# One kernel, several edits: w_in loaded and cast without a change of partitions, batch 1's queries in two loads, and a new order of small matmuls around chunk 0

## The chip, the cores and the metric

The kernel runs on one core of a Trainium2 chip. The metric is device time in microseconds (us). A core has five engines that run side by side, each through its own list of instructions in order: TensorE (PE in the profile; PEld is its weight load), VectorE (DVE), ScalarE (ACT), GpSimd (POOL) and SyncE (SP, which here only issues DMAs). An instruction waits on semaphores for what it needs, and everything behind it on its engine waits with it.

## What is computed

Two layers in a row, from inputs in float32. The first is a linear attention with cosine weights, for 8 batches, 8 heads, 576 positions and 64 features:

```python
r = np.maximum(x, 0.0); phi = np.concatenate([r * c, r * s], axis=-1)   # c, s: cos and sin of the position
q_p, k_p = phi(q), phi(k)
kv  = np.einsum('bhsf,bhsd->bhfd', k_p, v);  z = np.sum(k_p, axis=2)
num = np.einsum('bhsf,bhfd->bhsd', q_p, kv)
den = np.einsum('bhsf,bhf->bhs', q_p, z)[..., None] + 1e-06
attn = num / den
```

The second takes the 4608 tokens of 512 features that come out (heads side by side) through two matrices with a gate between them:

```python
h = x @ w_in                                   # 4608x512 by 512x2048
g = h * (1.0 / (1.0 + np.exp(-beta * h)))
out = g @ w_out                                # 2048x512
```

## The kernel before

**Attention.** A batch's q, k and v are each loaded as 128 partitions x 4 x 9 x 64 (`load_raw`, line 76). A partition holds nine neighbouring positions n of one head; the 128 partitions are 64 groups of positions for each of two heads (g), and the four blocks j are the other factor of the heads. Pairs of blocks make up a half jp of the heads. DVE or ACT takes the relu of q (`q_relu`) and k (`k_relu`) into bfloat16 and multiplies v by cosine and sine into `vb` (`v_scale`). The queries are turned, features to partitions, by PE transposes (`q_turn_pe`, batches 0 and 1) or by a DMA transpose on SP (`q_turn_dma`). Of the turned queries there are two sets: `qts`, a copy, and `qs`, the copy times the tangent of the position (`tan_mul`, with the table `tanr`), so that cosine and sine parts share one relu. PE then forms kv with 72 small matmuls of 64x64 tiles (`kv_mm`, L276), copied by `kv_take`, and the numerators and denominators with eight small matmuls for each n and jp (`num_mm`, L297). `x_rden` and `x_mul` divide (DVE, or ACT in `x_mul_act`), and the quotients are turned into `xt` by PE (`x_turn_pe`, L356) or DMA (`x_turn_dma`).

**The two matrices.** The tokens are cut into nine chunks of 512; a chunk is 8 blocks of 64 tokens, block 9b + n being position group n of batch b. So chunk 0 needs n = 0 to 7 of batch 0, chunk 1 needs n = 8 of batch 0 and n = 0 to 6 of batch 1. For each chunk PE makes 16 groups of 128 features (`h_mm`, L386, four matmuls of 512 columns that run over mi, the quarters of the 512 inputs: mi 0 and 1 come from half jp 0 of the heads, mi 2 and 3 from jp 1), ACT applies Silu out of PSUM (`h_act`, L394), and the second matrix follows: chunk 0 by 64 wide matmuls (`o_mm`, L544), chunk 1 by a seven-product scheme with half as wide matmuls (`o_fast`, L563), chunks 2 to 8 by orders that a planner has written (`ORDERS`), which the change leaves as they are. The scheme of seven products needs sums of weights T (`w_sums`) and of activations S1 to S4 (`g_sum`, L406) from DVE.

**Weights.** w_in comes in four stages of 512 columns, each 128 partitions x 4 x 512 float32 in one of four staging buffers; the partition of a row of w_in there is not the one that `xt` needs, since a 128-row block holds two g. `cast_win` (line 105) therefore casts to bfloat16 in pieces of 64 partitions, from partitions g*64 to partitions jj*64, on DVE, GpSimd or ACT. w_out follows in four stages through the same buffers (`load_w`), cast and scaled by 1/beta in 16 blocks (`cast_out`).

**The order.** All of it is written by hand, and each engine takes its instructions as the program issues them. DMAs of inputs are all issued on SP in one queue: q, v, k of batch 0 in halves, w_in stages 0 to 3, w_out 0 and 1, then batch 1's v, k, q, then w_out 2 and 3. Lines 685 to 754 are the attention for the first eight position groups of batch 0, with matmuls on zeros (`warm_pe`, `warm_long`) that keep PE occupied while data arrive. A loop over 32 slots follows (line 854): slots 0 to 15 are chunk 0's h groups, 16 to 23 the first half of the second matrix (eight of the 16 blocks, four at a time for each of four token rows), 24 to 31 the other half, one block at a time for all four. The dictionary `early` (line 807) hangs other work behind a slot: behind slot 4 the matmuls for n = 8 of batch 0 and `rest()`, which issues the casts and loads above; behind 22 batch 1's kv; behind 23 (`second`) the PE transposes of batch 1's queries; behind 25 and 26 the numerators for n = 0 to 6, one half of the heads each (a "seven": 56 small matmuls); behind 28 and 29 their turns. The loop of chunk 1 (line 882) has, behind slot 0, the numerators for n = 7 and 8 of batch 1, the relus and DMA turn of batch 2's queries, and the cosine half of its v; behind slot 4 its k, behind 6 the sums T, behind 10 its kv. Then come batch 3's query relus on ACT and their DMA turn (lines 899 to 901), and then `o_fast` (911), whose first step for each pair of rows is a product "1" and a copy by ACT, "c1" (L602), out of the bank in which product "6" goes on.

```python
    for slot in range(16):
        h_group(1, slot)
        if slot == 0:
            num_rest()
            att_q(2)
            v_half(2, 0)
...
    q_relu(3, 0, "act")
    q_relu(3, 1, "act")
    q_turn_dma(3)
...
    x, y = o_fast(1, 0, (2, 5, 4)), o_fast(1, 1, (3, 7, 6))
    ops(x, "1 c1")
```

Of the kernel before, what the change touches and what calls it, by code (L numbers as in the profile page):

```python
# [10 lines left out]
FP32 = mybir.dt.float32  # L11
# [5 lines left out]
P = 128  # L17
NQ = 9
# [4 lines left out]
def kernel(  # L23
# [52 lines left out]
    def load_raw(b, name, j0=0, j1=4):  # L76
        js = slice(j0, j1)
        src = {"q": q, "k": k, "v": v}[name][b]
        nc.sync.dma_start(  # L79
            out=raw_tile(b, name)[:, js].rearrange("q j n d -> q j (n d)"),  # L80
            in_=src.rearrange("(j g) (p n) d -> (g p) j (n d)", g=2, n=NQ)[:, js, :])
# [9 lines left out]
    w_in_v = moe_w_in.rearrange("(j p) f -> p j f", p=P)  # L91
# [3 lines left out]
    def load_w(kind, i, step=4):  # L95
# [3 lines left out]
        for a in range(0, 4, step):  # L99
            if kind == "out":  # L100
                nc.sync.dma_start(out=st[:, a : a + step], in_=w_out_v[:, 4 * i + a : 4 * i + a + step, :])
                continue
            nc.sync.dma_start(out=st[:, a : a + step], in_=w_in_v[:, a : a + step, i * 512 : (i + 1) * 512])

    def cast_win(i, gj, eng="dve", f0=0, f1=512, jps=slice(0, 2)):

        g, jj = gj
        o = win[i].rearrange("q (jp g) f -> q jp g f", g=2)[jj * HP : (jj + 1) * HP, jps, g, f0:f1]
        a = stages["in", i].rearrange("q (jp jj) f -> q jp jj f", jj=2)[g * HP : (g + 1) * HP, jps, jj, f0:f1]
# [16 lines left out]
    GJ = [(0, 0), (0, 1), (1, 0), (1, 1)]  # L126

    load_raw(0, "q", 0, 2)
    load_raw(0, "q", 2, 4)
    beta16 = const.tile([JT, P], FP32, name="beta16")  # L130
    nc.scalar.dma_start(out=beta16, in_=moe_beta.rearrange("(j p) -> j p", p=P))
# [63 lines left out]
    def q_relu(b, jp, eng="dve", n0=0, n1=NQ):  # L195
        return relu(qb[:, jp, n0:n1].rearrange("q n (j d) -> q j n d", j=2),
                    raw_tile(b, "q")[:, 2 * jp : 2 * jp + 2, n0:n1], eng)

    def k_relu(b, j0=0, j1=4, eng="dve", n0=0, n1=NQ):
        relu(rk.rearrange("q n j d -> q j n d")[:, j0:j1, n0:n1], raw_tile(b, "k")[:, j0:j1, n0:n1], eng)  # L200

    def v_scale(b, cs, jp=None, n0=0, n1=NQ, eng="dve"):
        t = (cos9, sin9)[cs]
        rv = raw_tile(b, "v")
        js = slice(0, 4) if jp is None else slice(2 * jp, 2 * jp + 2)
# [21 lines left out]
    def q_turn_pe(b, jp, bank, hold=False):  # L227

        parts = ((0, 0, 5), (1, 5, NQ))
# [40 lines left out]
    def kv_mm(b, jp, bank, jjs=(0, 1)):  # L270
        t = kv_out(jp, bank)
        for n in range(NQ):
            for jj in jjs:
                for g in range(2):
                    hs = slice(g * HP, (g + 1) * HP)
                    nc.tensor.matmul(  # L276
                        t[jj * HP : (jj + 1) * HP, g], lhsT=rk[hs, n, 2 * jp + jj, :],
                        rhs=vb[hs, n, 2 * jp + jj].rearrange("q s e -> q (s e)"),
# [10 lines left out]

    def num_mm(b, n, jp, bank, slot):  # L290

        for cs in range(2):
            for jj in range(2):
                rows = slice(jj * HP, (jj + 1) * HP)
                for g in range(2):
# [3 lines left out]
                        lhsT=(qts[b % 2], qs_of(b))[cs][rows, jp, n, cols],  # L299
# [385 lines left out]
    warm_pe(58, 48)  # L685
# [7 lines left out]
    for bank, n0, n1 in ((6, 0, 5), (7, 5, NQ)):  # L693
        nc.vector.tensor_copy(tanr[:, n0:n1, :].rearrange("q n p -> q (n p)"), ps[:, bank, 0 : (n1 - n0) * HP])
# [47 lines left out]
    for gj, eng in zip(GJ, ("pool", "dve", "pool", "dve")):  # L742
        cast_win(0, gj, eng, jps=slice(0, 1))
    for gj, eng in zip(GJ, ("act", "pool", "pool", "pool")):
        cast_win(0, gj, eng, jps=slice(1, 2))
# [10 lines left out]
    def cast_halves(i, fs=(0, 256)):  # L756
        for f in fs:
            for gj in GJ:
                cast_win(i, gj, "pool" if i > 1 and gj == GJ[3] else "dve", f, f + 256)

    cast_halves(1)

    def rest():

        cast_halves(2)
        cast_halves(3)
        x_mul(x_rden(2, 0, 8, NQ, (0, 1)), 8, NQ)
# [4 lines left out]
        load_raw(1, "q")  # L772
        load_w("out", 2, 2)
        load_w("out", 3, 2)
        x_turn_dma(0, 8, 9)
# [5 lines left out]
        q_relu(1, 0)  # L781
        q_relu(1, 1, n1=5)
# [6 lines left out]
    takes = []  # L789

    def second():

        takes.append(q_turn_pe(1, 0, 4, hold=True))
        takes.append(q_turn_pe(1, 1, 6, hold=True))
        cast_out(8)
        takes[0]("act", 0)
        takes[0]("dve", 1)
        cast_out(9, "a")
        takes[0]("dve", 0)
        takes[0]("act", 1)  # L800
        cast_out(10)
# [290 lines left out]
```

## Time and profile before

| | |
|---|---|
| median of 3 runs | 274.07 us (273.53 to 274.22) |
| the profiled execution | 274.44 us, of which the span is 272.7 us |
| PE busy | 265.3 us, 97% of the span |
| DVE, ACT, POOL busy | 224.0, 188.4, 68.3 us |
| DMA | 54.00 MB, mean 198 GB/s; 388 GB/s from 18.7 to 37.9 us |
| granted TensorE clock, mean | 0.998 |

The profile is one execution recorded by the hardware. Its timeline lists instructions with start, length, engine, line, shape and, in brackets, the idle time of the engine before them and what ended it; the chain of waits follows the work that ended last back from the end; the windows give each engine's busy time in a stretch. A PE row's length runs to the modelled end of its last matmul, so distances between starts say more about PE than lengths do. "L386" is line 386 of the kernel before.

### The profile page before, as it was taken

The page shows a single profiled execution, that of the slowest core. Times are in us where ns is not written, and L with a number is a line of the kernel's source. Part 1 is how long each engine was busy: PE and PEld are TensorE (multiplying, and loading weights), DVE is VectorE, ACT ScalarE, POOL GpSimd, SP SyncE. Part 2 cuts the span into 40 slices and gives each one's busy share as a digit, 9 for nine tenths or more (in the row PEclk, how much of TensorE's full clock was granted, in tenths as well). Part 3 has the DMA queues.
Part 4 walks back from the last instruction along what each step waited for, and adds up shares of the span by engine and source line. Part 5 has one row for each costly group of instructions (what it writes and reads, how often), then busy time and mean ns, then how long its engine had stood idle before and what let it go on. Part 6 is the DMA issues. An engine that isn't in the chain of part 4 may idle for free.

```text
span 272.7 us, 8970 instructions
## 1 busy us (share of the span) xinstructions
PE 265.3 (97%) x3712; PEld 206.8 (76%) x3712; DVE 224.0 (82%) x596; ACT 188.4 (69%) x384; POOL 68.3 (25%) x89
## 2 busy tenths in 40 slices
PE   8899999999899999999999999999999999999994
PEld 8554455455784588888888888888888888888883
DVE  5989969499989889789989997899589768757852
ACT  4778777796419656899489966996696179428920
POOL 1444000510078000660085009300840060000001
PEclk9999999999999999999999999999999999999999
DMA  6999999999969999994589439943600570015005
GB/s 237 374 395 383 392 390 319 379 201 336 284 130 311 240 348 226 240 313 103 147 216 370 92 58 223 332 71 62 181 2 2 61 185 1 2 27 130 0 2 155
DMA packets 50681, 54.00 MB, mean 198 GB/s; under 512 B 31232, under 2 KB 31760, under 8 KB 50640
## 3 DMA queue, kind: packets, MB, share of 16 engines
q1 hardware_dynamic: 47504, 45.55, 59.1%
q0 software_dynamic: 2784, 7.61, 9.6%
q8 instruction: 29, 0.48, 0.7%
q10 hardware_dynamic: 352, 0.27, 0.4%
q14 instruction: 12, 0.10, 0.1%
HBM read 36.71 MB, written 9.44 MB: 169 GB/s over the span
## 4 chain that ended last, share of the span: by engine, by line
PE 85%; DVE 9%; DMA 3%; SPq 1%; issue 1%; ACT 1%; DVEq 0%
PE ps L621 32%; PE ps L511 27%; PE ps L386 10%; PE ps L544 5%; PE ps L563 4%; PE ps L297 3%; DMA raw_v<-in_v_dram 3%; PE ps L276 3%; DVE vb L219 1%; DVE xs L319 1%; DVE qs L223 1%; SPq L79 1%; DVE S L406 1%; DVE rk L193 1%; DVE qb L193 0%
## 5 line engine op out<-in xcount | busy, mean ns | idle before, releaser
L537 POOL DMA_DIRECT2D out_dram<-o_sb x58 | 33.9, 591 | 147.3 <-ACT o_sb L658 86.3
L420 ACT ACTIVATE g_t<-ps,beta 128x512 bf16<-128x512 f32 x96 | 60.3, 702 | 1.4 <-PE ps L511 1.3
L621 PEld LDWEIGHTS <-S 128*128 128x128 bf16 x448 | 43.4, 98 | 5.2
L511 PE MATMUL ps<-w_stage 128*128 128x256 bf16 x288 | 46.6, 272 | 0.1
L386 PE MATMUL ps<-xt,win 128*128 128x512 bf16 (+1 forms) x196 | 42.8, 375 | 0.1
L511 PEld LDWEIGHTS <-w_stage 128*128 128x128 bf16 x384 | 37.3, 98 | 5.1 <-issue 0.2
L487 DVE TENSOR_TENSOR ps<-ps,p 128x256 f32<-128x256 f32 x74 | 30.5, 428 | 8.6 <-PE ps L511 3.0
L394 ACT ACTIVATE g_t<-ps,beta 128x512 bf16<-128x512 f32 x48 | 32.3, 688 | 7.2 <-PE ps L386 7.1
L621 PEld LDWEIGHTS <-g_t 128*128 128x128 bf16 x336 | 32.3, 98 | 4.5 <-ACT g_t L420 0.4
L386 PEld LDWEIGHTS <-win 128*128 128x128 bf16 x196 | 18.7, 98 | 21.1 <-issue 0.5
L511 PE MATMUL ps<-xt,win 128*128 128x256 bf16 x192 | 32.9, 273 | 0.0
L511 PEld LDWEIGHTS <-win 128*128 128x128 bf16 x288 | 28.0, 98 | 3.4
L621 PE MATMUL ps<-wout,g_t 128*128 128x256 bf16 x224 | 28.9, 273 | 0.0
L406 DVE TENSOR_TENSOR S<-g_t 128x512 bf16<-128x512 bf16 (+1 forms) x66 | 25.7, 418 | 3.3 <-ACT g_t L420 1.7
L480 ACT COPY ps<-ps 128x256 f32<-128x256 f32 x62 | 22.6, 383 | 7.5 <-PE ps L621 4.0
L217 ACT ACTIVATE vb<-raw_v,sin 128x256 bf16<-128x256 f32 (+1 forms) x58 | 26.0, 503 | 1.5 <-DMA raw_v<-in_v_dram 1.5
L621 PE MATMUL ps<-T,S 128*128 128x256 bf16 x224 | 26.6, 273 | 0.0
L621 PE MATMUL ps<-wout,S 128*128 128x256 bf16 x224 | 26.4, 273 | 0.0
L319 DVE TENSOR_TENSOR xs<-ps,rden 128x768 bf16<-128x768 f32 (+4 forms) x26 | 22.8, 884 | 0.9 <-DVE rden L312 0.2
L223 POOL TENSOR_TENSOR qs<-qt,tanr 128x1152 bf16<-128x1152 bf16 x6 | 14.3, 2387 | 27.4 <-PE ps L563 21.0
L658 ACT COPY o_sb<-ps 128x512 f32<-128x512 f32 x11 | 6.3, 587 | 20.1 <-PE ps L621 20.1
L487 DVE TENSOR_TENSOR ps<-ps,u 128x256 f32<-128x256 f32 x36 | 15.3, 427 | 5.3 <-PE ps L511 3.3
(112 smaller groups left out, 414.7 us busy)
## 6 DMA issues: line engine op xcount, KB each, us to landing
raw_v<-in_v_dram SPq DMA_DIRECT2D x7, 1152.0 KB, 9.7
raw_k<-in_k_dram SPq DMA_DIRECT2D x7, 1152.0 KB, 9.5
raw_q<-in_q_dram SPq DMA_DIRECT2D x7, 1152.0 KB, 7.4
out_dram<-o_sb POOLq DMA_DIRECT2D x58, 128.0 KB, 4.5
w_stage<-in_moe_w_in_dram SPq DMA_DIRECT2D x3, 1024.0 KB, 12.8
w_stage<-in_moe_w_out_dram SPq DMA_DIRECT2D x2, 1024.0 KB, 7.9
w_stage<-in_moe_w_out_dram SPq DMA_DIRECT2D x4, 512.0 KB, 11.9
out_dram<-o_sb SPq DMA_DIRECT2D x10, 128.0 KB, 2.4
```

The costliest lines, as they stand in the source:

```text
L217: got = nc.scalar.activation(o, a, AF.Copy, scale=t[:, n : n + 1])
L223: return eng.tensor_tensor(dst.rearrange("q n (g p) -> q n g p", g=2), src.rearrange("q n (g p) -> q n g p", g=2), tanr[:, n0:n1].unsqueez ...
L319: nc.vector.tensor_tensor(o.rearrange("q j n s d -> q j (n s) d"), nv[:, :, a:z, :, 0:D].rearrange("q j n s d -> q j (n s) d"), rden[:, :, ...
L386: nc.tensor.matmul(ps[:, h_bank(c, jt), i * 64 : (i + w) * 64], lhsT=win[jt // 4][:, mi, (jt % 4) * P : (jt % 4 + 1) * P], rhs=xt[:, i : i ...
L394: return nc.scalar.activation(gs[c, jt // 4][:, jt % 4], ps[:, h_bank(c, jt)], AF.Silu, scale=beta[:, jt : jt + 1])
L406: return nc.vector.tensor_tensor(o, l, r, op=op)
L420: return nc.scalar.activation(gs[c, jt // 4][:, jt % 4], bank, AF.Silu, scale=beta[:, jt : jt + 1])
L480: return nc.scalar.copy(at("a", 0), at("b", 0))
L487: nc.vector.tensor_tensor(dst, at("b", 0), st["p5"], op=ALU.add)
L511: nc.tensor.matmul(dst, lhsT=l[:, g], rhs=r[:, :, g * HP : (g + 1) * HP], start=start and g == 0, stop=g == 1, skip_group_check=True)
L537: (eng or own).dma_start(out=out_v[bb, n][:, m0:m1], in_=o_sb[hf * HP : (hf + 1) * HP, m0:m1])
L621: nc.tensor.matmul(dst, lhsT=l(i), rhs=r[:, i], start=start and i == 0, stop=i == order[-1], skip_group_check=True)
```

## The change

- **w_in.** A half jp now holds heads blocks j = jp and jp + 2, no longer 2jp and 2jp + 1 (`heads`, and the slices in `q_relu`, `k_relu`, `v_scale`, `kv_mm`). With that, a partition of a staged w_in row is the one that `xt` needs, if rows are taken as (jj, mi, d): each load becomes two, for 64 partitions each, and a cast runs over all 128 partitions. Stage 0 is cast by mi (GpSimd, DVE, ACT, GpSimd), stages 1 to 3 in four pieces of 128 columns each, all on DVE.
- **Batch 1's queries** come in two loads (n below 7, then 7 and 8), between halves of w_out stages 2 and 3. Only n = 0 to 6 are turned by PE, 7 and 8 by two DMA transposes and two GpSimd products behind slot 31.
- **Bursts and turns of chunk 0.** The matmuls for n = 8 of batch 0 move from slot 4 to slot 22, directly before batch 1's kv; batch 1's query turn moves from 23 to 25, both sevens to 27, their turns to 30 and 31. The loads of batch 2 and the last w_out casts move with them.
- **Chunk 1.** The first halves of groups 0 to 3 are issued ahead of the loop. The numerators n = 7 and 8 of batch 1 move from slot 0 to slot 10, directly before batch 2's kv, and their division behind it; batch 2's query relus move from slot 0 to slot 4.
- **Batch 3's query relus** and turn move behind the two "1 c1" of `o_fast`.
- **The start.** A DMA on ACT's queue reads 8 numbers of each of 16 rows spread over v of batch 0 ("early rows of v"), ahead of beta's. 74 matmuls on zeros stand first, not 58. The table `tanr` is copied by ACT, not DVE.

The core of the diff:

```diff
+    def heads(j0, j1):
+        if j1 - j0 == 4:
+            return slice(0, 4)
+        at = 2 * (j0 % 2) + j0 // 2
+        return slice(at, at + 1) if j1 - j0 == 1 else slice(at, 4, 2)
...
-            nc.sync.dma_start(out=st[:, a : a + step], in_=w_in_v[:, a : a + step, i * 512 : (i + 1) * 512])
+            for jj in range(2):
+                nc.sync.dma_start(out=st[jj * HP : (jj + 1) * HP, a : a + step],
+                                  in_=w_in_v[jj, :, a : a + step, i * 512 : (i + 1) * 512])
...
-        o = win[i].rearrange("q (jp g) f -> q jp g f", g=2)[jj * HP : (jj + 1) * HP, jps, g, f0:f1]
-        a = stages["in", i].rearrange("q (jp jj) f -> q jp jj f", jj=2)[g * HP : (g + 1) * HP, jps, jj, f0:f1]
+        o, a = win[i][:, mi0:mi1, f0:f1], stages["in", i][:, mi0:mi1, f0:f1]
...
+    touch = const.tile([2 * H, 8], FP32, name="touch")
+    nc.scalar.dma_start(out=touch, in_=v[0].rearrange("h (s r) d -> (h s) r d", s=2)[:, 0, 0:8])
     nc.scalar.dma_start(out=beta16, in_=moe_beta.rearrange("(j p) -> j p", p=P))
...
-        parts = ((0, 0, 5), (1, 5, NQ))
+        parts = ((0, 0, 5), (1, 5, NQ)) if b == 0 else ((0, 0, 4), (1, 4, 7))
...
-    warm_pe(58, 48)
+    warm_pe(74, 48)
...
-        nc.vector.tensor_copy(tanr[:, n0:n1, :].rearrange("q n p -> q (n p)"), ps[:, bank, 0 : (n1 - n0) * HP])
+        nc.scalar.copy(tanr[:, n0:n1, :].rearrange("q n p -> q (n p)"), ps[:, bank, 0 : (n1 - n0) * HP])
...
-    for gj, eng in zip(GJ, ("pool", "dve", "pool", "dve")):
-        cast_win(0, gj, eng, jps=slice(0, 1))
-    for gj, eng in zip(GJ, ("act", "pool", "pool", "pool")):
-        cast_win(0, gj, eng, jps=slice(1, 2))
+    for mi, eng in enumerate(("pool", "dve", "act", "pool")):
+        cast_win(0, mi, mi + 1, eng)
...
-        load_raw(1, "q")
-        load_w("out", 2, 2)
-        load_w("out", 3, 2)
-        x_turn_dma(0, 8, 9)
+        load_w("out", 2, 2, 0, 2)
+        load_raw(1, "q", n1=7)
+        load_w("out", 2, 2, 2, 4)
+        load_w("out", 3, 2, 0, 2)
+        load_raw(1, "q", n0=7)
+        load_w("out", 3, 2, 2, 4)
...
+    def eighth():
+        for jp in range(2):
+            num_mm(0, 8, jp, 4, jp)
+        kv_mm(1, 0, 6)
+        kv_mm(1, 1, 6)
+        kv_take((0, 1), 6, "act")
+        x_mul(x_rden(4, 0, 8, NQ, (0, 1)), 8, NQ)
...
     early = {
-        4: lambda: (num_mm(0, 8, 0, 2, 0), num_mm(0, 8, 1, 2, 1), rest()),
+        4: rest,
         15: lambda: (v_scale(1, 1, n1=8, eng="act"), k_relu(1, 2, 4, "act")),
-        22: lambda: (kv_mm(1, 0, 6), kv_mm(1, 1, 6), kv_take((0, 1), 6, "act"), q_relu(1, 1, "act", 5)),
-        23: second,
-        25: lambda: (num_seven(0, 4), x_mul(x_rden(4, 0, 0, 7, (0,)), 0, 7), cast_out(13)),
-        26: lambda: (num_seven(1, 6), x_mul(x_rden(6, 0, 0, 7, (1,)), 0, 7)),
-        28: lambda: x_turn_pe(1, 0, 7, 4, ("act",), (0,)),
-        29: lambda: x_turn_pe(1, 0, 7, 5, ("dve",), (1,)),
+        22: eighth,
+        25: turn,
+        27: sevens,
+        30: lambda: x_turn_pe(1, 0, 7, 4, ("act",), (0,)),
+        31: lambda: (x_turn_pe(1, 0, 7, 5, ("dve",), (1,)), q_rest()),
     }
...
+    for jt in range(4):
+        h_mm(1, jt, (0, 1))
     for slot in range(16):
-        h_group(1, slot)
+        if slot < 4:
+            h_mm(1, slot, (2, 3))
+            h_act(1, slot)
+        else:
+            h_group(1, slot)
         if slot == 0:
-            num_rest()
-            att_q(2)
             v_half(2, 0)
...
         if slot == 4:
+            att_q(2)
             k_all(2)
...
         elif slot == 10:
+            num_rest()
             kv_all(2, eng="act")
+            x_rest()
...
-    q_relu(3, 0, "act")
-    q_relu(3, 1, "act")
-    q_turn_dma(3)
...
     ops(x, "1 c1")
     one_sums(1)
     ops(y, "1 c1")
+    q_relu(3, 0, "act")
+    q_relu(3, 1, "act")
+    q_turn_dma(3)
```

`turn` holds the turn of batch 1's queries, their takes, the remaining relus and the loads of batch 2's v, q and k; `sevens` both sevens and their divisions; `q_rest` the two DMA transposes and two GpSimd products for n = 7 and 8; `rest` as before, without what has moved. The small matmuls for n = 8 of batch 0 read a copy of their tangent queries that GpSimd makes (`qs_last`), as batch 1's turn writes the tile that holds them.

## The prediction

> **What bounds the kernel now.** I read the busy time by windows first, then TensorE's (PE's) timeline, then the chain of waits. The windows divide the span where PE's behaviour changes; their columns are stretch, length, busy time (and instructions) of PE, PEld, DVE, ACT, POOL, then the granted clock, DMA share and GB/s.
>
> ```profile
> 18.70:37.90 19.20, 19.20 (x110) 8.96 (x110) 17.10 (x42) 15.90 (x27) 2.91 (x4) 1.00 1.05 388
> 37.90:52.00 14.10, 14.09 (x291) 8.15 (x291) 8.62 (x17) 9.53 (x17) 1.19 (x2) 1.00 1.06 356
> 52.00:69.10 17.10, 17.10 (x292) 9.45 (x290) 16.96 (x34) 13.97 (x23) 3.54 (x7) 1.00 1.06 290
> 69.10:70.20 1.10, 0.14 (x12) 0.15 (x2) 1.03 (x4) 1.10 (x3) 0.00 (x0) 1.00 1.05 396
> 70.20:269.00 198.80, 198.72 (x2696) 168.59 (x2695) 164.99 (x462) 135.84 (x291) 52.94 (x60) 1.00 0.59 148
> ```
>
> From 18.7 us on PE never rests, but for one hole at 69.1. So only three things can pay: an earlier 18.7, that hole, and PE work or slow changes inside "busy" time. An engine made faster elsewhere pays nothing. DMA is full (1.05 to 1.06) until 70, so data come at a fixed pace and PE, if it gets ahead, can run into them.
>
> The hole, in PE's and ACT's timelines (start, length, what, idle before and what ended it):
>
> ```profile
> 65.91 1.91 PE L563 MATMUL ps<-wout,g_t 128*128 128x256 bf16 x16
> 70.15 1.91 PE L563 MATMUL ps<-T,S 128*128 128x256 bf16 x16 [0.96 <-ACT p L602]
> ...
> 67.62 2.22 ACT L192 ACTIVATE qb<-raw_q 128x1152 bf16<-128x1152 f32 x2 [0.82 <-DMA raw_q<-in_q_dram]
> 69.74 0.63 ACT L602 COPY p<-ps 128x256 f32<-128x256 f32 x2
> ```
>
> ACT waits for batch 3's queries, takes 2.22 for their relus, and only then does the two copies for which PE stands.
>
> Inside busy time the slow changes show in the starts. PE, chunk 1's first group and the rest:
>
> ```profile
> 50.36 1.03 PE L386 MATMUL ps<-xt,win 128*128 128x512 bf16 x4
> 51.70 8.81 PE L386 MATMUL ps<-xt,win 128*128 128x512 bf16 x40
> ```
>
> The first-to-first distance is 1.34; four 512-wide matmuls at 0.216 are 0.86, so the burst of 32 small matmuls (64x64 tiles, num_mm) between them cost 0.48. The chain of waits prices them:
>
> ```profile
> 22.07 0.25 PE ps L297 x16
> ...
> 42.98 0.58 PE ps L297 x56
> 43.56 0.97 PE ps L544 x4
> 44.53 0.18 PE ps L297 x5
> 44.70 0.01 issue
> 44.71 0.61 PE ps L297 x40
> ```
>
> 56 cost 0.58 there and 16 cost 0.25: 0.0083 each. So 32 are worth 0.27, and **0.21 of the 0.48 is going into 64x64 tiles and back**. The first 56 confirm it: 41.09 to 43.49 less eight wide ones (1.73) leaves 0.67 = 0.46 + 0.21. The second 56, 43.49 to 45.25 less four wide ones, leaves 0.90: **0.22 more, a stall**, in which the rows at 44.53 and 44.71 are split; its qs pieces come from DVE at 44.0.
>
> **The change, part by part.**
>
> *Merged bursts.* Before there are six small bursts from 22 to 62: n=8 of batch 0 (slot 4), kv of batch 1, two sevens, n=7,8 of batch 1, kv of batch 2. After, n=8 stands directly before kv, the two sevens together, n=7,8 directly before the second kv: three bursts. Gain 3 x 0.21 = **0.63**. A change between two kinds of small matmul is not shown alone; bounds 0 and 0.21 each, I take 0, as they share the tile size.
>
> *The second sevens' stall* (**0.22**) goes: they now run after slot 27, two slots (1.73) behind the transposes instead of two split ones, and the takes are 384 and 512 wide, not 640 and 512. By ACT's and DVE's rows (0.5 to 0.6 each) the last take ends near 44.6, PE comes near 44.7. What is late next is ACT's cast of row block 15, near 47.2; PE wants it near 48.3.
>
> *Four transposes fewer* in batch 1's turn (14, not 18): 18 start 0.0565 apart, so **0.23**. They become two DMA transposes on SP and two GpSimd products (2.39 for 1152 columns, so some 0.5 for 256), issued behind loads of batch 2, needed only after slot 10 of chunk 1 near 59. Batch 2's k, ahead of them, lands near 54. On SP they delay batch 2's turn, whose relus end near 54 anyway.
>
> *The hole* (**1.00**: 2.39 from the first of 144 small matmuls to 70.15, less 1.24 for them and 0.15 to leave). The relus of batch 3 stand behind both copies now. Next in line is S2 (L406). DVE's run of 14.7 us before S1, from 51.92 to 66.66, began behind n=7,8; now it can begin near 50.1, when the last xt copy is done, so S2 ends near 67.7 and PE comes near 68.1. Batch 3's DMA turn is issued near 69.3 against 69.86, so the DMAs behind it on SP are no later.
>
> *Four half-groups of chunk 1 first*: same matmuls. ACT gets its Silus 0.43 apart but takes 0.69, and falls 1 to 2 us behind; four banks cover that.
>
> *Casts.* DVE's 22 of 0.50 between 10 and 35 become 13, with as many columns each. DVE had 1 to 2 us in hand for each w_in stage, so this is worth 0, except one: two casts end at 16.83, behind num_mm, and one will not; at most 0.1.
>
> *The start.* Rows of DVE's timeline:
>
> ```profile
> 7.12 1.42 DVE L223 TENSOR_TENSOR qs<-ps,tanr 128x512 bf16<-128x512 bf16 x2
> 9.16 1.34 DVE L209 TENSOR_TENSOR vb<-raw_v,ps 128x1152 bf16<-128x1152 f32 x1
> 12.25 1.35 DVE L209 TENSOR_TENSOR vb<-raw_v,ps 128x1152 bf16<-128x1152 f32 x1 [0.19 <-DMA raw_v<-in_v_dram]
> ```
>
> DVE is busy from 7.12 to 15.6 but for 0.19, so earlier rows of v can pay 0.19 at most, though v's first half lands 2.70 behind q's (4.84, 6.30, 9.00, 10.44 for q, q, v, k). The touch costs: a second issue on ACT (0.45) shifts the table load, sine and tangent, so the tangent transposes start near 4.0, not 3.56. The 16 more dummies, 0.040 apart, end at 3.95 and are hidden by this; the second ones behind it end 0.45 later, the first turn at 7.54, not 7.08, and DVE's product starts at 7.58. That is 0.46 on DVE's run; its 0.19 of idle time takes a part. Moving tanr to ACT (idle 2.10 there) frees DVE earlier, where it only waits. Less the cast's 0.1, PE's dense work begins **0.17 later** (0.46 - 0.19 - 0.10). Bounds: 0.5 later (the full delay), 0.3 earlier (no delay, idle and cast both gone).
>
> *Queries in two loads, casts of w_out reordered*: q's 7 rows land near 39.8 behind k (36.1) and half a w_out stage; turned near 41.8. Hidden by 1 us.
>
> *w_in by two loads of 64 partitions.* No load of before has 64 partitions, only stores. In the packet records, a 2,048-byte packet of a w_in load takes 0.085 at the median, one of SP's 64-partition stores 0.151; GpSimd's 64-partition stores take 0.159 for 4,096 bytes, the full pace. So between 0 and 0.066 for each of the 128 packets that an engine has of w_in: **0 to 8.4 us** late for all that lands behind. I take 0, by the many GpSimd stores and because a load, unlike the stores after 240, has the next load queued behind it, so engines may be in different halves; both ends stay in the range.
>
> **Sum.** -0.63 - 0.22 - 0.23 - 1.00 + 0.17 = -1.91. The profiled execution took 274.44 (span 272.7 and 1.74 around it): 272.53. It lies 0.37 above the median of the runs, 274.07; on that, **272.2 us** (272.16).
>
> **Rivals.**
>
> *A, slower: half pace on w_in.* At 0.151 k of batch 1 lands 8.4 late, at 44.5; its relu and the burst, at 37.90 against a landing of 36.13, follow at 46.2, 8.3 late; the gains behind it (1.0, 0.23, 0.22, 0.42) stay: 274.07 + 8.3 - 1.9 = 280.5. It decides from 0.3 (PE's slack at this burst) plus 2 us, so from packets of 0.103 on the average. For it: SP's store rows; against: GpSimd's. [...] Mixed halves give 274 to 277.
>
> *B, gains lost in waits.* PE comes earlier to data of unchanged pace: k's relu ends at 37.56, PE wants it near 37.8. If it lands 0.5 later, or the start's 0.5 is paid whole, or small kinds do cost their change, 0.6 to 1.2 is lost: 272.9 to 273.5.
>
> *C, the start is bound by landings after all*: v's excess of 1.26 over its neighbours' 1.44 then comes off, 270.9 to 271.6. DVE's rows speak against it.
>
> **Chances.** Forecast (271.6 to 272.9) 0.52, A 0.22, B 0.20, C 0.06. A measurement of this kernel can tell some 0.3%, 0.8 us. Faster by more: the forecast, C and half of B, 0.68; within: the other half, 0.10; slower: A, 0.22. The range of 8 in 10 leaves out C's end and most of A: 271.3 to 275.5.
>
> **What will show it.** Right: no hole of PE near 68, w_in packets of 0.085, stage 3 landed by 25, PE busy from 18.8 on, three small bursts. Wrong: the last w_in landing past 27, a wait of PE for rk or win casts, the dense stretch beginning past 19.2.

## The result and the profile after

| | before | after |
|---|---|---|
| median | 273.77 us (6 runs, 273.28 to 274.22) | 288.64 us (6 runs, 287.16 to 290.33) |
| after / before | | 1.0544 (95%: 1.0504 to 1.0584) |
| the profiled execution | 274.44 us, span 272.7 | 289.28 us, span 287.5 |
| PE busy | 265.3 us, 97% | 267.7 us, 93% |
| idle time of PE, up to the end of its last matmul | 3.7 us | 15.7 us |

Ratios compare fast runs, those within 1.5% of the fastest of the same kernel, while medians hold all runs (`e6_buffer` has one run outside, `e15_half` two).

The change makes the kernel 14.9 us slower. PE has hardly more to do; it waits. The windows of the kernel after (stretch, length, busy time of PE, PEld, DVE, ACT, POOL, granted clock, DMA share, GB/s); the second, third and last line begin at the same places of its work as the first, second and last that the prediction shows of before:

```profile
9.00:18.70 9.70, 6.55 (x213) 3.90 (x213) 7.00 (x17) 5.97 (x15) 3.10 (x3) 0.82 1.04 269
18.70:46.30 27.60, 21.32 (x120) 9.48 (x118) 12.03 (x34) 16.43 (x30) 0.96 (x2) 1.00 1.06 294
46.30:58.40 12.10, 12.06 (x248) 7.16 (x249) 7.91 (x18) 8.34 (x16) 0.00 (x0) 1.00 1.07 342
58.40:78.16 19.76, 16.89 (x173) 8.08 (x170) 13.80 (x26) 13.70 (x25) 6.67 (x10) 1.00 1.02 258
78.16:82.37 4.21, 3.45 (x160) 2.86 (x160) 4.21 (x8) 2.88 (x5) 0.00 (x0) 1.00 1.05 400
82.37:284.00 201.63, 199.55 (x2696) 168.42 (x2696) 168.27 (x468) 135.91 (x291) 52.98 (x60) 1.00 0.60 146
```

The second line, up to batch 1's kv, is 27.6 long where before had 19.2, with 6.3 idle. Its DMA share is as full as before's (1.06 and 1.05), but the DMAs move 294 GB/s, not 388: each is busy all the time and brings less. The fourth line, chunk 1, has 2.9 more of idle time. The last line is 2.8 longer than before's: 1.4 is one wait (at 120.85, for DVE), 0.6 lies behind PE's last matmul.

What PE waits for stands in DVE's timeline: the casts of w_in for stages 1, 2 and 3, then batch 1's k, each begin when a landing allows it (the brackets: idle time before, and what ended it):

```profile
24.79 1.43 DVE L121 CAST win<-w_stage 128x512 bf16<-128x512 f32 x4 [5.23 <-DMA w_stage<-in_moe_w_in_dram]
29.52 1.43 DVE L121 CAST win<-w_stage 128x512 bf16<-128x512 f32 x4 [3.29 <-DMA w_stage<-in_moe_w_in_dram]
34.35 1.43 DVE L121 CAST win<-w_stage 128x512 bf16<-128x512 f32 x4 [3.40 <-DMA w_stage<-in_moe_w_in_dram]
...
45.49 0.76 DVE L199 TENSOR_SCALAR rk<-raw_k 128x1152 bf16<-128x1152 f32 x1 [0.29 <-DMA raw_k<-in_k_dram]
...
67.24 1.91 DVE L199 TENSOR_SCALAR qb<-raw_q 128x1152 bf16<-128x1152 f32 x2 [5.50 <-DMA qt<-qb]
```

The last piece of w_in lands at 34.26 (24.51 before), batch 1's k at 45.47 (36.13). The last line is a second cause, which the prediction did not see: batch 2's query relus write `qb`, and batch 1's positions 7 and 8 lie in that buffer until two DMA transposes have read them. DVE stands still for 5.50 us.

The hole that the change was to close is closed; ACT's timeline has both copies ahead of the relus:

```profile
79.23 0.38 ACT L612 COPY p<-ps 128x256 f32<-128x256 f32 x1 [0.83 <-PE ps L573]
80.10 0.37 ACT L612 COPY p<-ps 128x256 f32<-128x256 f32 x1 [0.50 <-PE ps L573]
80.37 2.22 ACT L198 ACTIVATE qb<-raw_q 128x1152 bf16<-128x1152 f32 x2
```

### The profile page after: what moved, and what is told of

Same layout as the page of the kernel before. It is cut to its first block, busy times and chain, and to the rows that moved or that the text cites. A ratio compares the mean times of both kernels' runs of the same rounds, so it can differ in the third digit from the quotient of the medians.

```text
span 287.5 us, 9001 instructions
## 1 busy us (share of the span) xinstructions
PE 267.7 (93%) x3724; PEld 206.3 (72%) x3724; DVE 218.5 (76%) x585; ACT 189.0 (66%) x388; POOL 65.9 (23%) x85
## 4 chain that ended last, share of the span: by engine, by line
PE 65%; DMA 24%; DVE 7%; issue 1%; SPq 1%; ACT 1%; DVEq 0%
PE ps L631 27%; PE ps L521 26%; DMA w_stage<-in_moe_w_in_dram 10%; PE ps L396 6%; DMA w_stage<-in_moe_w_out_dram 5%; DMA qt<-qb 4%; DMA raw_v<-in_v_dram 3%; PE ps L573 3%; PE ps L306 2%; PE ps L283 2%; DVE qs L230 1%; DMA raw_q<-in_q_dram 1%; DVE vb L226 1%; DVE S L416 1%; SPq L86 1%
## 5 line engine op out<-in xcount | busy, mean ns | idle before, releaser
L230 POOL TENSOR_TENSOR qs<-qt,tanr 128x1152 bf16<-128x1152 bf16 (+1 forms) x8 | 16.7, 2090 | 31.2 <-DVE den L318 20.8
L226 DVE TENSOR_SCALAR vb<-raw_v,cos 128x256 bf16<-128x256 f32 x63 | 20.7, 378 | 2.8 <-DMA raw_v<-in_v_dram 2.8
```

What stands on the lines that cost most here:

```text
L226: got = nc.vector.tensor_scalar(o, a, scalar1=t[:, n : n + 1], scalar2=None, op0=ALU.mult)
```

## The experiments

All times are medians, each against the kernel before on the same chip (273.35 to 273.66).

### Is it the 64 partitions, or the number of loads?

`e1_halves` is before with its w_in loads cut in two by partitions; `e2_columns` has as many loads, all over 128 partitions.

```diff
e1  -  nc.sync.dma_start(out=st[:, a : a + step], in_=w_in_v[:, a : a + step, ...])
    +  for hf in range(2):
    +      ph = slice(hf * HP, (hf + 1) * HP)
    +      nc.sync.dma_start(out=st[ph, a : a + step], in_=w_in_v[ph, a : a + step, ...])
e2  -  load_w("in", 0, 2)  ...  load_w("in", i)
    +  load_w("in", 0, 1)  ...  load_w("in", i, 2)
```

> The kernel before with one edit: every load of w_in is split into two, one for partitions 0 to 63 and one for 64 to 127; casts, order and the rest are untouched. Theory 1 (loads of 64 neighbouring partitions run at half pace, and that is the first loss): the 2,048-byte packets of w_in take 0.15 to 0.16 us instead of 0.085, the last piece of w_in lands near 33 to 34 instead of 24.5 and batch 1's k near 44 to 45.5 instead of 36.1, kv of batch 1 starts 7 to 9 later, and the time is 280 to 283. Theory 2 (the number of loads costs, not their partitions): slower too, but the packets keep 0.085 and gaps between loads appear. Theory 3 (the new order of small matmuls and loads is what costs): packets near 0.085 to 0.10 and a time within 1 us of before, 274 to 275.

> The kernel before with twice as many loads of w_in, as many as in the changed kernel, each over all 128 partitions and half of the row blocks. Theory 1 (64 partitions): nothing changes, packets 0.085, last piece of w_in near 24.5, time 274.0 +- 0.5. Theory 2 (number and size of the loads): as slow as the kernel with loads by 64 partitions, 280 to 283. Theory 3 (the new order): 274.0 +- 0.5, as theory 1.

Measured: `e1_halves` 283.71, 1.0372 (1.0349 to 1.0394), 10.4 slower; `e2_columns` 273.50, 1.0001 (0.9991 to 1.0010). One line of windows from each, for 18 to 24 us; first e1, then e2:

```profile
18.00:24.00 6.00, 5.62 (x50) 2.78 (x41) 2.48 (x8) 3.81 (x8) 1.83 (x3) 0.83 1.05 216
```

```profile
18.00:24.00 6.00, 5.99 (x52) 3.11 (x50) 5.03 (x12) 5.01 (x9) 1.41 (x3) 1.00 1.05 387
```

The DMA share is the same, the rate is 216 against 387. The 2,048 packets of w_in (2,048 bytes each) take 0.153 at the median in e1, 0.084 in e2, 0.085 in before, 0.160 in the kernel after. The last piece of w_in lands at 33.93 in e1, k at 45.14. So the partitions alone cost 10.4, a little over the upper end of theory 1, and the number of loads nothing.

`e5_ports` asks which 64 partitions.

```diff
+    load(t1, 0, P, 0, 2); load(t1, 0, P, 2, 4)          # 128 partitions
+    load(t2, 0, HP); load(t3, 0, HP); load(t2, HP, P); load(t3, HP, P)
+    load(t4, 32, 96); load(t5, 32, 96)
+    for t in (t6, t7): load(t, 0, HP); load(t, HP, P, eng=nc.scalar)
```

> The kernel before, and behind its end seven extra loads' worth of w_in into free buffers, so its time has no meaning and only the packets and landings of the extra loads are read; all are 0.5 MB per load. In order on SP: two loads over 128 partitions, two over partitions 0 to 63, two over 64 to 127, two over 32 to 95, then two pairs of 0 to 63 on SP and 64 to 127 on ACT's queue. Theory 1a (half pace, because 64 neighbouring partitions as such share something with the next load of the same half): packets 0.085 for 128 partitions and 0.15 for all three kinds of halves; 0.085 to 0.10 for the pairs on two queues if both halves then run side by side, 0.15 if they do not. [...] Theory 2 (number or size of loads): all eight kinds alike.

Its windows while the extra loads run; in order 128 partitions, 0 to 63, 64 to 127 (SP's and ACT's queue both had that half at work), 32 to 95:

```profile
273.00:274.00 1.00, 0.00 (x0) 0.00 (x0) 0.00 (x0) 0.00 (x0) 0.00 (x0) 0.50 1.05 408
275.00:279.00 4.00, 0.00 (x0) 0.00 (x0) 0.00 (x0) 0.00 (x0) 0.00 (x0) 0.50 1.05 203
283.00:287.00 4.00, 0.00 (x0) 0.00 (x0) 0.00 (x0) 0.00 (x0) 0.00 (x0) 0.50 1.06 203
292.00:293.00 1.00, 0.00 (x0) 0.00 (x0) 0.00 (x0) 0.00 (x0) 0.00 (x0) 0.50 1.03 381
```

The packets take 0.084, 0.169, 0.171 and 0.085. It isn't the number 64: the middle 64 partitions run at nearly the pace of 128 (381 GB/s against 408), either half runs at half (203). What makes the halves differ from the middle is not shown. So theory 1a, 0.15 for all three kinds, fails by the 0.085 of the middle, and theory 2 by the 0.169 and 0.171 of the halves; the "64 neighbouring partitions" of the expectations, and the 64 of the prediction, hold for the two halves, not for any 64. (The pairs on two queues did not meet: ACT's halves were through when SP's began.)

`e12_twoq` (the changed kernel, batch 1's queries as before, upper halves of w_in on ACT's queue) lets the halves run together. As built, it puts the upper halves of all four stages there; its expectation names stages 0 and 1 only.

```diff
-            for jj in range(2):
-                nc.sync.dma_start(...)
+            for jj in jjs:
+                (nc.sync, nc.scalar)[jj].dma_start(...)
...
     k_relu(0, 0, 2, "act", 0, 5)
+    load_w("in", 1, jjs=(1,))
```

> The changed kernel with batch 1's queries as before, and with the upper halves (partitions 64 to 127) of w_in's stages 0 and 1 loaded on ACT's queue beside the lower halves on SP's; stages 2 and 3 keep both halves on SP. Theory 1 (two halves at a time use the DMAs whole, one at a time only half): packets near 0.085 to 0.10 while both queues run, stage 1 complete near 19 to 21 where the changed kernel has 24.7, then half pace again for stages 2 and 3, 5 us late instead of 9.8; 280 to 283. Rival (a load of 64 partitions is slow whatever runs beside it): packets 0.15 throughout, stage 1 complete near 24, 285 to 287.

Measured: 283.32, 1.0345 (1.0313 to 1.0377). Two of its windows:

```profile
18.00:20.00 2.00, 0.03 (x4) 0.06 (x1) 0.43 (x1) 0.13 (x1) 0.86 (x1) 0.88 1.10 221
...
24.00:26.00 2.00, 2.00 (x15) 1.44 (x14) 1.25 (x4) 1.07 (x2) 0.00 (x0) 0.67 1.06 350
```

From 18 to 20 nearly all packets are of ACT's queue, the upper half (202 against 6), and take 0.162; from 24 to 26 both halves are at work (144 and 198), at 0.096. So halves help each other when both are moving, but the two queues drift apart, and in the first of these windows one half moves almost alone. Stage 1 is complete at 24.66, not by 21: the time is 0.3 over theory 1's range, and its landings are late. Of the 5.2 that this kernel gains on the kernel after, some 2.9 are batch 1's queries (below), so the second queue saves about 2 of w_in's 10.

`e7_one` and `e8_onebuf` were to load the changed kernel's rows over 128 partitions at once (`e8_onebuf` with the repair of `e6_buffer`, below).

```diff
-            for jj in range(2):
-                nc.sync.dma_start(out=st[jj * HP : (jj + 1) * HP, a : a + step], in_=w_in_v[jj, :, a : a + step, ...])
+            for mi in range(a, a + step):
+                nc.sync.dma_start(out=st[:, mi], in_=w_in_v[:, :, mi, ...])      # (jj d) against jj, d
```

> The changed kernel with one edit: each quarter mi of a w_in stage is loaded by one load over all 128 partitions (16 loads of 256 KB), no longer by two loads of 64 partitions for several quarters; the same numbers land in the same places, and all else stands. Theory 1 (loads of 64 neighbouring partitions run at half pace): packets 0.085, the last piece of w_in lands near 25 instead of 34.3, and the time is that of the kernel without the w_in edits, 277.5 to 279, 10 less than the changed kernel. Rival (the rows of w_in in the order jj, mi, d are slow to read, however many partitions a load has): packets 0.15, 287 to 289.

> The changed kernel with both repairs: one load of 128 partitions for each quarter of a w_in stage, and batch 1's last query relus in a place of their own. If the two losses are apart from each other, 275.0 to 276.5, some 12 to 13 below the changed kernel and still 2 above before; what then stays is the start, the wait of PE with no releaser near 20, and order. If chunk 1's loss was only a result of late data, the second repair brings nothing on top of the first, 277.5 to 279.

Measured: 349.02 and 347.29, 1.2764 and 1.2698: a miss by 70 us, and no test of theory 1. The window of e7:

```profile
20.00:60.00 40.00, 13.28 (x43) 5.22 (x43) 3.41 (x11) 7.34 (x13) 0.96 (x2) 0.57 0.13 51
```

The packets take 0.084 again, but the DMA share is 0.13, as two busy engines of 16 would give, and the rate 51 GB/s. The source's first dimension is jj there, with two steps. That this dimension leaves two engines is the author's reading; no run changes it alone.

### Chunk 1: the two DMA transposes

`e3_rest` has every edit but those of w_in.

> The changed kernel with w_in loaded and cast as before (128-partition loads, the old pairing of head blocks, casts of 64 partitions); all other edits stand. Theory 1, with the wait found in the changed kernel's trace (batch 2's query relus stand on DVE behind the two DMA transposes that read the same buffer, and those behind loads of batch 2 on SP): packets 0.085, w_in landed near 24.5, PE dense from about 18.8, and DVE idle before batch 2's first query relu for 1 to 4 us; 272.2 if PE does not notice that, 273.5 to 275.5 if it does. Theory 3 (the order, whatever the loads): 283 to 287, with the wait as long as in the changed kernel, 5.5.

Measured: 278.26, 1.0198 (1.0166 to 1.0230). That is between the ranges of the two theories. So w_in is 10 of the 14.9, and the other edits cost 4.9 where the prediction gave them a gain of 1.9. `e6_buffer` gives batch 1's positions 7 and 8 a place of their own; `e9_queries` undoes the whole part.

```diff
e6  -  q_relu(1, jp, "act", 7)
    +  relu(q_last[:, jp]..., raw_tile(1, "q")[..., 7:], "act")          # q_last lies in S3
    -  ... in_=qb[:, jp, 7:]..., transpose=True
    +  ... in_=q_last[:, jp]..., transpose=True
e9  -  load_raw(1, "q", n1=7)  ...  load_raw(1, "q", n0=7)
    +  load_raw(1, "q")                    # behind k; q_turn_pe turns all nine positions
    -  31: lambda: (x_turn_pe(...), q_rest()),
    +  31: lambda: x_turn_pe(...),
```

> The kernel that has all edits but those of w_in (278.3), with the relus of positions n = 7 and 8 of batch 1's queries put into a place of their own, in a buffer of sums that is not yet in use, so that batch 2's query relus need not wait until the two DMA transposes have read them. If that wait is what the order costs in chunk 1: DVE starts batch 2's queries when they land, near 53.1, not at 56.9, the four holes of PE at 60.4, 67.4, 70.0 and 71.7 (1.7 us together) go or nearly go, and so do slower steps between them; 275.6 to 276.8. If DVE is late for another reason (GpSimd's two products beside it, batch 2's k landing at 56.5), the holes stay and the time stays within 0.6 of 278.3.

> The kernel with all edits but those of w_in (278.3), with batch 1's queries also as before: one load behind k, all nine positions turned by PE (18 transposes), no DMA transposes and GpSimd products for n = 7 and 8. Theory 1 now: the two extra DMA transposes are what chunk 1 pays for, first by the buffer they read, then (with a buffer of their own, 277.7) because batch 2's k lands at 57.9 beside them, 2.6 later than before, while the DMAs move 26 to 84 GB/s from 55 to 58. Without them k lands near 55, the three holes of PE at 66.9, 69.5 and 71.2 go, and the time falls to 273.0 to 274.5. Rival: DVE is late because of the order alone (the division of n = 7 and 8 stands behind the sums T and ahead of the products, on the path of the first product 6); then the holes stay and the time is 276.5 to 278.

Measured: `e6_buffer` 277.65, 1.0150 (1.0109 to 1.0191); `e9_queries` 275.64, 1.0073 (1.0045 to 1.0101), again between what its theory and its rival gave. DVE's timeline of e3, then e6:

```profile
56.93 1.91 DVE L195 TENSOR_SCALAR qb<-raw_q 128x1152 bf16<-128x1152 f32 x2 [3.23 <-DMA qt<-qb]
```

```profile
53.31 1.43 DVE L195 TENSOR_SCALAR qb<-raw_q 128x1152 bf16<-128x1152 f32 x2
57.89 1.36 DVE L195 TENSOR_SCALAR rk<-raw_k 128x2304 bf16<-128x2304 f32 x1 [3.16 <-DMA raw_k<-in_k_dram]
```

The repair takes 0.8 off (4.9 to 4.1) and moves the wait, as large, to the next load: batch 2's k. The windows of e6 and e9 from 55 to 58 show what holds it:

```profile
55.00:58.00 3.00, 3.00 (x16) 1.35 (x15) 0.11 (x1) 3.00 (x8) 0.35 (x1) 1.00 0.34 56
```

```profile
55.00:58.00 3.00, 3.00 (x15) 1.37 (x14) 3.00 (x6) 3.00 (x7) 3.00 (x4) 1.00 0.81 228
```

With the two transposes among loads and stores the DMAs move 56 GB/s there, without them 228. The share of 0.34 doesn't mean idle DMAs, as a window counts a packet where it begins: from 54 to 55 of e6, 479 of the transposes' packets of 256 bytes begin and nine packets of stores that take 2.8 us on the average, and by what overlaps with each us from 55 to 58 the share is 1.0 to 1.6. Batch 2's k lands at 57.87 in e6, at 56.09 in e9. PE's waits near 67 to 72 (1.24 us in e6) are gone in e9. The part costs 2.9 (4.9 less 2.0, each against its own before). The pair e6 and e9 shows it for the part as a whole, split loads and GpSimd products with it; that the transposes hold up the DMAs is read from these packets, and by what means they do isn't settled.

### The start

```diff
e10  +  touch ...; warm_pe(74, 48); nc.scalar.copy(tanr...)     # all three
e13  -  warm_pe(58, 48)
     +  warm_pe(74, 48)                                          # this alone
e14  +  touch ...; nc.scalar.copy(tanr...)                       # the other two
```

> The kernel before with the start's edits alone: the small read of v on ACT's queue, 74 matmuls on zeros for 58, and the table of tangents copied by ACT. By the prediction 0.27 later (0.46 of the small read's issue on DVE's run, less 0.19 of idle time), 273.8 to 274.0 against 273.6; bounds 0.5 later and 0.3 earlier. By the traces of the kernels that have it, wide matmul 0 starts 0.5 later and number 10 near 0.1 later, and PE then waits 0.3 to 0.7 near 19.7 with no releaser shown; if that wait comes with the start's edits, 274.2 to 274.6.

> The kernel before with 74 matmuls on zeros instead of 58, nothing else. The three edits of the start together cost 2.7 (276.4 against 273.7). Theory of blocks: in every trace PE's waits without a releaser stand where the running number of its instructions is the same modulo 256, and PE goes on 1.3 to 1.5 us after a single packet of 16 KB on the instruction queue; 16 more matmuls with their weight loads are 32 instructions, which shift the blocks against the program, to places where the packet comes late. Then this kernel shows the waits near 44 (0.5) and near 155 (0.2 to 0.9), and its median is 274.3 to 275.8. Rival: the small read and ACT's copies are what costs; then 273.5 to 273.9, with PE's first turn a little earlier.

> The kernel before with the small read of v on ACT's queue and the table of tangents copied by ACT, and 58 matmuls on zeros as before. Theory of blocks: no wait of PE without a releaser, and only the start's own delay, 273.6 to 274.2. Rival: the read and the copies cost most of the 2.7, 275 to 276.5.

Measured: all three 276.40, 1.0103 (1.0078 to 1.0128); the matmuls alone 275.47, 1.0061 (1.0046 to 1.0075); read and copies alone 273.82, 1.0011 (0.9997 to 1.0024). The first is 1.8 above the highest figure expected of it, the other two are what the theory of blocks gave. PE's timeline of e13:

```profile
19.97 1.37 PE L386 MATMUL ps<-xt,win 128*128 128x256 bf16 x9 [0.55 <-issue]
...
44.52 0.22 PE L297 MATMUL ps<-kv,qt 64*64 64x65 bf16 x3 [0.62 <-issue]
...
155.70 0.92 PE L621 MATMUL ps<-T,S 128*128 128x256 bf16 x7 [0.99 <-issue]
```

Three waits that nothing releases ("issue"), 2.2 us together, and 16 matmuls at the start set them off, the last of them 150 us later. Counted in the trace (matmuls and weight loads in order of start), PE goes on at instructions 706, 1216 and 4541; divided by 256 they leave 194, 192 and 189. In nine other traces there are 11 more such waits of 0.1 to 2.5 us, and all leave 191 to 194. The instruction queue of the profile brings 29 packets of 16 KB in a span, one for each 256 of PE's 7,400 instructions, and PE goes on 1.3 to 1.5 us after the latest of them is through (18.48, 43.21 and 154.17 here). All this fits a program that comes to PE in blocks of 256 instructions, one to a packet, and PE having run to the end of a block before the next was there. That is a reading of these counts and packets; no run shows the blocks otherwise, and a block's end, below too, is a place of this count. Thirty-two more instructions at the start, 16 matmuls with their weight loads, put the blocks' ends elsewhere. A wait of 0.16 near 39 in six kernels is not of this kind (it stands at other numbers). One wait each in e7 and e8 (0.57 and 0.74) leaves 194 too, but 5.3 and 5.1 after the packet; these two the account doesn't cover.

### Do merged bursts pay?

```diff
e4   -  (batch 3's query relus and turn ahead of o_fast)
     +  (the same three lines behind the second "1 c1")
e11  the order of after alone: loads, casts, batch 1's queries and start as before
e15  e11, and  -  load_raw(1, "q")  load_w("out", 2, 2)
               +  load_w("out", 2, 2, 0, 2)  load_raw(1, "q")  load_w("out", 2, 2, 2, 4)
e16  e4, and the sevens together behind slot 26, num_rest() before kv_all(2) at slot 10
e17  e4, and n = 8 of batch 0 before batch 1's kv, the sevens together behind 26, turn behind 24
e18  e4, and the sevens together behind slot 26
```

> The kernel before with one edit: batch 3's query relus and their DMA turn stand behind the two first copies of the seven-product scheme, as in the changed kernel. If every execution of before has PE's hole of 0.96 us there, as its profiled one has (274.44), the time falls by 0.7 to 1.0, to 272.4 to 272.8 against 273.4. Rival: the hole is in that execution alone, because batch 3's queries landed late in it (ACT waited 0.82 for them); the profile of the kernel with twice as many loads of w_in has no hole there and lies 1.27 lower. Then the median falls by 0 to 0.3.

> The kernel before with the order of bursts and turns alone: merged bursts, chunk 1's first four half-groups ahead, batch 2's and batch 3's relus moved; loads and casts of w_in, batch 1's queries and the start are as before. By the prediction's terms three merged bursts give 0.63 and the second sevens' stall 0.22, so 0.6 to 0.9 below before, 272.6 to 273.0, if no wait takes their place. Rival: the holes of chunk 1 stay, because the order itself puts DVE's work there on the path; 275 to 277.

> The kernel with the order of bursts and turns alone (274.7), with the first half of w_out's stage 2 loaded ahead of batch 1's queries. That kernel has a wait of PE for a cast of w_out at 40.3 (0.71), because its merged bursts bring PE to the second matrix before that half lands at 40.5. If this wait is what eats the gain of the merged bursts, it goes and the time is 273.9 to 274.2, the queries landing 1.4 later without harm; if the queries then come late to their turn, the wait moves there and the time stays at 274.5 to 275.

> The kernel before with two of the three merged bursts and the later relus of batch 3, and no other edit: both sevens behind slot 26, the numerators n = 7 and 8 directly before batch 2's kv with their division behind it. The measured gains of these merges are 0.18 (1.34 for the two sevens apart, 1.16 together) and 0.22 (1.72 and 1.50). If nothing takes their place, 0.4 below before, 273.2; if the division of n = 7 and 8, now in the middle of DVE's run, makes the first product 6 late, 273.6 to 274.3.

> The kernel before with the two merged bursts of chunk 0 (n = 8 of batch 0 directly before batch 1's kv, both sevens together, batch 1's turn one slot later) and the later relus of batch 3; chunk 1 as before, so that the blocks of PE's instructions there stay where they were. Measured gains of these merges: 0.22 and 0.18. Theory of blocks: no block's end falls into a late packet, and the time is 0.2 to 0.4 below before, 273.1 to 273.3; a wait of PE for w_out's cast near 40 would take it back. Rival (merged bursts bring nothing to the time, wherever they stand): 273.5 to 274.5.

> The kernel before with the two sevens together behind slot 26, their turns a slot later, and the later relus of batch 3: one merge alone, worth 0.18 by the bursts' length (1.34 apart, 1.16 together). Theory of blocks: 273.3 to 273.5, no wait of PE near 70, where the kernel with this merge and that of chunk 1 has 2.46 without a releaser. Rival (the merge of the sevens itself sets off that wait): 274.5 to 276.5.

| | median | against before (95%) |
|---|---|---|
| e4_hole | 273.67 | 1.0001 (0.9991 to 1.0011) |
| e11_bursts | 274.74 | 1.0039 (1.0025 to 1.0052) |
| e15_half | 274.89 | 1.0039 (1.0018 to 1.0059) |
| e16_two | 274.70 | 1.0053 (1.0033 to 1.0073) |
| e17_early | 275.19 | 1.0061 (1.0047 to 1.0075) |
| e18_sevens | 273.39 | 1.0000 (0.9986 to 1.0015) |

e4 came as its rival said, e15 and e18 in their ranges (e18 without a gain); e11 lies between its two, e16 and e17 above both of theirs.

e4 gains nothing. The profile of e2, whose program has the old order there, explains it; ACT's timeline:

```profile
66.59 2.21 ACT L192 ACTIVATE qb<-raw_q 128x1152 bf16<-128x1152 f32 x2
68.70 0.63 ACT L602 COPY p<-ps 128x256 f32<-128x256 f32 x2
```

There batch 3's queries came in time, the relus began at 66.59 and not at 67.62, and PE has no hole. The hole of 0.96 belonged to the one execution that was profiled, 0.67 above its median: of six other profiles with the old order there, five (e1, e2, e5, e13, e14) have none, and e10 has 0.34.

The bursts themselves got shorter as predicted. From the last wide matmul before a burst to the first behind it, less that matmul: n = 8 and kv 0.35 + 1.24 apart, 1.37 together; the sevens 0.67 + 0.67 (e4), 1.16; n = 7, 8 and kv 0.48 + 1.24, 1.50: 0.22, 0.18 and 0.22. (In e9 and e11 the sevens together take 1.43 and gain nothing.) It doesn't reach the time. In e17, PE's timeline:

```profile
41.60 1.02 PE L544 MATMUL ps<-wout,g_t 128*128 128x512 bf16 x4 [2.05 <-DVE wout L123]
...
44.30 1.02 PE L544 MATMUL ps<-wout,g_t 128*128 128x512 bf16 x4 [0.67 <-ACT wout L121]
```

Without the turn between, PE comes to the second matrix before w_out's stage 2 is there and cast (in e11 it lands at 40.48; in e17 DVE begins the cast at 41.07, behind the division of n = 8 that the merge puts there). And in e16, inside the burst of 144 in `o_fast`, PE's timeline and then the DMA queues of 68.2 to 69.5:

```profile
70.73 0.26 PE L297 MATMUL ps<-kv,qt 64*64 64x65 bf16 x1 [2.46 <-issue]
```

```profile
q1 hardware_dynamic: 223, 0.49, 100.9%
q8 instruction: 1, 0.02, 5.3%
```

The one packet of instructions came through at 69.43 among 223 packets of loads, and PE went on 1.3 later. By the count the block ends at the same instruction of the same burst in before, near 68.7, where the packet was through at 66.32: the merge does not move this end, the packet is late. What the merge moves is the block's end two before this one, from 52.8 to 59.2, and the two packets behind that begin at 61.95 and 68.33, not at 53.63 and 65.42; that the late packets follow from it isn't tested. The wait is also not the whole price: measured as the bursts are, `o_fast` with its burst takes 17.88, in e4 13.69, and of the 4.2 between them the wait is 2.46; the rest falls into 70.69 to 74.10, where the granted clock was 0.50. e15's profile has the same wait, 1.93; its executions range from 273.67 to 279.19, so the wait is hardly in all of them. e18 leaves chunk 1 alone and has no such wait there, but its 0.18 can't be seen in the time: in its trace the sevens take 1.21, and batch 1's kv 1.47 instead of 1.24, with the wait of 0.16 near 39. None of these kernels is faster than before.

## Why the prediction was wrong, point by point

The forecast was 272.2 and a range of 271.3 to 275.5; measured 288.6. Four parts, each from medians against before on the same chip, add up to the change: w_in 10.4 (e1); batch 1's queries 2.9 (e3 less e9); the start 0.9 on top of the new order (e9 less e11; 2.7 alone, e10); the order 1.1 (e11). Together 15.3, measured 14.9. Each part carries a spread of up to 1 us, and the start shows that parts depend on each other, so the closeness of the sum is partly luck.

- **w_in by 64 partitions: the step that failed.** "I take 0", between 0 and 8.4. The runs show the upper end, and more: packets of 0.153 instead of 0.085, 9.4 us later landings, 10.4 in the time. Two reasons were given for 0. That engines would be in different halves is wrong for loads that follow one another in one queue (e1, 0.153) and right only while both halves move (e12, 0.096). The other, that GpSimd's 64-partition stores keep the full pace, was a misreading: in before, the store that runs alone from 138.19 has 32 packets with a median of 0.307 for 4,096 bytes, half the pace (0.296 to 0.311 in six other profiles), and 0.159 is found where stores of both halves follow close on each other. So GpSimd's rows agree with SP's store rows, which bounded the cost from above. That the mixing of halves gives the 0.159 was not tried.
- **Rival A** had the mechanism and most of the size: 8.3, where e1, which is this mechanism alone, measured 10.4. What it had wrong, with the forecast, is the rest: -1.9 assumed, +4.9 measured (e3).
- **Four transposes fewer** is right for PE: 1.05 (e4) or 1.00 (e9) to 0.78 (e3, e6), 0.22 to 0.27 for a predicted 0.23. "They become two DMA transposes ... needed only after slot 10" failed: their cover was looked for at their readers, and not at the buffer they read, nor at the DMAs they run among. It costs 2.9.
- **The hole, 1.00: failed.** It was in the profiled execution; closing it is worth 0 in the median (e4). The prediction had noted that the profile lay 0.37 above the median and drew nothing from it.
- **The second sevens' stall, 0.22**: the same; the second seven takes 0.67 in e1, e2 and e4.
- **Merged bursts, 0.63**: right in the bursts (0.62 at best), wrong in the sum. What stood behind them was not asked: w_out's landing near 40.5 and its cast (e11, e17), and the wait without a releaser inside the burst of 144 (2.46, e16). In the time the order costs 1.1.
- **The start, 0.17 later**: read and copies measured 0.30 (-0.1 to 0.7), which agrees in size but also with nothing. The 16 matmuls, "hidden", cost 1.95 (e13).
- **Casts**: nothing to see; DVE waits for landings (3.29 to 5.23 us ahead of the casts of stages 1 to 3). The casts' share was not measured alone.
- **Chunk 1's half-groups first**: in the order's 1.1, not measured alone.

## What to carry to other kernels

Look at the partitions that a load reaches and at its source's first dimension, and not only at its bytes: in e5 the lower or the upper 64 partitions alone doubled a packet's time (0.169 and 0.171 against 0.084) and the middle 64 did not (0.085), and in e7 loads whose source had a first dimension of two kept the DMAs at a share of 0.13, where the loads of before have 1.05 (that the dimension is the cause is not shown). When a step is moved to a DMA, look for who next writes the buffer that it reads (DVE stood 5.50 us for it in the kernel after), and for the loads that are at work beside it (batch 2's k landed at 57.87 in e6, at 56.09 in e9). A gain read from one execution counts only if other executions have the wait too, and an edit that adds or moves PE's instructions ahead of short bursts needs a new profile of the whole span, for "issue" waits far behind it (0.99 at 155.70 in e13, from 16 matmuls at the start).

## What the runs showed that I had not expected

- The instruction queue brings 29 packets of 16 KB in a span, one for each 256 of PE's instructions, and in 14 places over ten traces PE stands at the same place of that count (189 to 194 left over) for 0.1 to 2.5 us and goes on 1.3 to 1.5 after the packet. In these places PE used up a block, mostly of small matmuls, in 2.7 to 8.3 us (the wait left out), and the packet began 0.3 to 5.8 us after PE had entered that block. Full DMAs are not a condition: near 158 in e3 and 163 in e12 their share was 0.12 and 0.14 while the packet moved. Why a packet comes late in one execution and not in another is open.
- The granted clock was 0.82 from 9 to 18.7 in the kernel after, 1.00 before: 0.50 from 12.10 to 15.51, behind a wait of PE of 2.06 that ended at 11.46. In e16 and e15 it was 0.50 for 3.41 us from 70.69 and from 71.77, where waits of 2.46 and 1.93 ended at 70.73 and 70.85. But from 18.7 to 46.3 in the kernel after, with 6.3 us idle, it was 1.00, so what lowers it isn't shown.
